# One load moved behind a group of DMA transposes: the sixth batch's v in a fused attention and mixer kernel

## The chip, the cores and the metric

The kernel runs on one core of a Trainium2 chip. The metric is device time in microseconds (us) of one execution; lower is better. Batches are numbered from 0 below, as in the code: the fifth batch is batch 4, the sixth is batch 5.

## The reference

For each of 8 batches and 8 heads (576 rows, head size 64) a linear attention with position weights is computed, then a mixer with two pairs of weights over all heads:

```python
phi(x) = concat(relu(x) * cos_w, relu(x) * sin_w)       # per row
kv  = phi(k).T @ v ;  z = sum(phi(k))
x   = (phi(q) @ kv) / (phi(q) @ z + 1e-6)               # 576 x 512 per batch, heads side by side
h   = relu(x.T @ w_tok1) @ w_tok2 ;  u = x + h.T        # token mixing, 576 -> 256 -> 576
out = u + relu(u @ w_ch1) @ w_ch2                       # channel mixing, 512 -> 1536 -> 512
```

## The kernel before

The 576 rows of a batch lie on 128 partitions in five pieces (j = 0 to 4); four are full and the fifth fills half of the partitions, two batches sharing one tail tile. Batches 0 and 1 and the preparation for 2 and 3 follow a list written out by hand. From batch 2 on there is a regular loop, one period for each batch p: the channel mixing of batch p (`channel`, L576 to L611) is TensorE's main work, and other batches' steps are hung into it at numbered slots. There are 12 slots after the first products (L589, tile `c_ps`) and 8 after the half sums of the second ones (L606, tile `o_ps`). In period p, `hooks_for(n, m, nxt)` hangs in:

- for batch n = p + 1: the kv product (slot 0, L361), the five numerators and their division (`numf`, L390, tile `nf`, slots 2 to 6; the division on DVE, L409 to L413), the token mixing (slots 7 to 8, L433), and the making of u (slots 10 to 12: `um` L460 and the addition L465 on DVE, the cast `ubc` to `ub` on POOL, the DMA transpose `utx` of `ub` into `uT`, L472, on SP; at slot 12 the tail, whose transpose for odd batches is L503)
- for batch m = p + 2: the casts of v to bf16 (`cast`, L264, on POOL, slots 3 to 7), the features of q on ACT (slots 9 to 13) and of k on DVE (slots 13 to 17), L330 and L332, and the DMA transposes `turnx` of the q features into `qpT`, L354 on SP: pieces 0 and 1 at slot 12, 2 and 3 at slot 15, 4 at slot 16
- for batch nxt = p + 3: the loads of k and q (slot 0) and of v (slot 9), L143 on SP, two DMAs each (512 and 640 KB), one for the even and one for the odd partitions

The stores of the output (L621, SP) come inside the second half of the channel mixing, two DMAs after j = 1 (between slots 14 and 15) and two after j = 3.

The order of calls is the order on each engine and queue: the schedule is manual, only the waits are put in by the framework. So SP issues its DMAs strictly in this order and each waits for its own data or buffer. Raw k and q have two buffers each, raw v one (L135 and below: `raw[t, 0 if t == "v" else b % 2]`), so a v load waits until the casts of the batch before it have read the buffer. `uT` and `qpT` have two buffers each.

Of the kernel before, what the change touches and what calls it, by code (L numbers as in the profile page):

```python
# [58 lines left out]
def kernel(  # L59
# [580 lines left out]
    def hooks_for(n, m, nxt):  # L640

        h = {}

        def at(slot, f, *a):
            h.setdefault(slot, []).append(lambda: f(*a))
        if nxt is not None:
            at(0, load, nxt, "k")
            at(0, load, nxt, "q")
            at(9, load, nxt, "v")
        if n is not None:  # L650
            at(0, n.kv_all)
            for j in range(JA):
                at(2 + j, n.num_all, j)
            for j in range(JA):
                at(7 + j // 3, n.mix, j, 2)
            at(8, n.mix_out)
            for g in range(3):
                at(10 + g, n.u_all, g)
        if m is not None:
            for j in range(JA):  # L660
                at(3 + j, m.cast, j, 1, 2, "P")
                at(9 + j, m.q_feature, j)
                at(13 + j, m.k_feature, j)
            at(12, m.turnx, 0, 2)
            at(15, m.turnx, 2, 2)
            at(16, m.turnx, 4, 1)
        return h

    evac = ["A"] * 7 + ["D", "A", "D", "D", "D"]
    for p in range(2, B):  # L670
        s = bt[p]
        n = bt[p + 1] if p + 1 < B else None
        m = bt[p + 2] if p + 2 < B else None
        nxt = p + 3 if p + 3 < B else None
        channel(s.uT, s.u, store_batch(p), evac if n else ["A", "D"] * 6, hooks_for(n, m, nxt))
# [33 lines left out]
```

## Time and profile before

| what | value |
|---|---|
| five runs | 274.94, 274.39, 274.09, 276.79, 274.52 us |
| median | 274.52 us |
| profiled execution | 274.94 us, of which the span of instructions is 273.2 us |
| busy in the span | PE 262.7, DVE 173.7, ACT 111.0, POOL 47.8 us |
| granted TensorE clock | 1.00 |
| DMA | 53.37 MB, mean 195 GB/s; 66.2% of 16 engines' span on SP's queue |

The periods of p = 2, 3, 4 and 5 start at 88.65, 116.24, 144.91 and 172.50 us of the span. All times inside the kernel below are counted from the start of the span. PE is TensorE's matmul, PEld its weight load, DVE VectorE, ACT ScalarE, POOL GpSimd; SPq is the queue of SyncE, whose times are those of issuing a DMA and not of its transfer. A DMA's landing is given as the time from issue to landing. Matmuls are pipelined, so the profile's durations of neighbours overlap a little.

### The profile page before, as it was taken

How to read it: one execution, taken by the hardware profiler on the slowest of the kernel's cores; microseconds unless marked ns; L12 is line 12 of the kernel's file. 1: busy time of each engine (PE TensorE's matmuls, PEld its weight loads, DVE VectorE, ACT ScalarE, POOL GpSimd, SP SyncE). 2: the span in 40 equal slices, each digit the busy share in tenths (PEclk: the TensorE clock that was granted, in tenths of full speed). 3: DMA queues.
4: the chain of work that ended last, by engine and by line, in shares of the span. 5: the costliest groups of instructions: out<-in, count | busy, mean ns of one | idle time of the engine just before them, and what ended most of it. 6: DMA issues, size and time to landing. Idle time of an engine off the chain costs nothing.

```text
span 273.2 us, 4855 instructions
## 1 busy us (share of the span) xinstructions
PE 262.7 (96%) x1923; PEld 137.9 (50%) x1941; DVE 173.7 (64%) x346; ACT 111.0 (41%) x176; POOL 47.8 (17%) x67
## 2 busy tenths in 40 slices
PE   6988999999999999999999999999999999999994
PEld 2775556455444644454445544554455444444443
DVE  6389788899982658945794669476837643424422
ACT  2786372565490548052903390339133201301300
POOL 2173060040060043500350026002000210000000
PEclk9999999999999999999999999999999999999999
DMA  6999999999999999999999958900980062012012
GB/s 205 358 233 174 288 229 254 356 175 248 382 220 220 317 382 359 195 218 302 334 179 241 352 164 179 230 30 3 219 204 2 0 155 97 0 46 107 2 66 89
DMA packets 79079, 53.37 MB, mean 195 GB/s; under 512 B 47824, under 2 KB 76496, under 8 KB 79056
## 3 DMA queue, kind: packets, MB, share of 16 engines
q1 hardware_dynamic: 74512, 48.77, 66.2%
q0 software_dynamic: 4144, 3.77, 9.1%
q10 hardware_dynamic: 400, 0.52, 0.5%
q8 instruction: 15, 0.25, 0.4%
q14 instruction: 8, 0.07, 0.1%
HBM read 35.85 MB, written 9.44 MB: 166 GB/s over the span
## 4 chain that ended last, share of the span: by engine, by line
PE 89%; DMA 5%; DVE 4%; issue 1%; DVEq 0%
PE o_ps L606 25%; PE c_ps L589 25%; PE c L512 8%; PE o L524 7%; PE b L433 6%; PE u L460 5%; PE kv L361 3%; DMA kt<-in_k_dram 3%; PE nf L390 3%; DMA qpT<-qp 2%; PE ut L488 1%; PE tr L345 1%; DVE kp L332 1%; PE o_ps L598 1%; PE nm L390 1%
## 5 line engine op out<-in xcount | busy, mean ns | idle before, releaser
L268 ACT ACTIVATE h<-c_ps 128x512 bf16<-128x512 f32 x52 | 31.0, 597 | 108.9 <-PE c_ps L589 65.3
L606 PE MATMUL o_ps<-wc,h 128*128 128x512 bf16 x317 | 71.5, 379 | 0.4
L589 PE MATMUL c_ps<-uT,wc 128*128 128x512 bf16 x288 | 70.4, 379 | 0.0
L606 PEld LDWEIGHTS <-h 128*128 128x128 bf16 x324 | 31.7, 98 | 38.2
L589 PEld LDWEIGHTS <-wc 128*128 128x128 bf16 x336 | 30.8, 98 | 32.6
L270 DVE TENSOR_SCALAR h<-c_ps 128x512 bf16<-128x512 f32 x32 | 22.0, 688 | 28.4 <-PE c_ps L589 28.4
L264 POOL CAST ub<-u 128x1024 bf16<-128x1024 f32 x14 | 14.9, 1067 | 108.6 <-issue 64.2
L330 ACT ACTIVATE qp<-qt,cos_t 128x512 bf16<-128x512 f32 x33 | 23.1, 713 | 11.8 <-DMA qt<-in_q_dram 11.5
L264 POOL CAST vbf<-vt 128x512 bf16<-128x512 f32 (+3 forms) x28 | 19.5, 731 | 48.0 <-DMA vt<-in_v_dram 46.7
L609 DVE TENSOR_TENSOR u<-o_ps,u 128x512 f32<-128x512 f32 x24 | 16.5, 688 | 17.5 <-PE o_ps L606 17.4
L512 PE MATMUL c<-uT,wc 128*128 128x512 bf16 x96 | 22.7, 379 | 0.1
L524 PE MATMUL o<-wc,h 128*128 128x512 bf16 x92 | 21.6, 379 | 0.2
L413 DVE TENSOR_TENSOR x<-nf,den 128x512 bf16<-128x512 f32 x30 | 20.7, 691 | 1.0
L332 DVE TENSOR_SCALAR kp<-kt,cos_t 128x512 bf16<-128x512 f32 x30 | 17.9, 599 | 5.5 <-DMA kt<-in_k_dram 5.5
L330 ACT ACTIVATE qp<-qt,sin_t 128x512 bf16<-128x512 f32 x30 | 21.1, 711 | 0.0
L465 DVE TENSOR_TENSOR u<-u,x 128x1024 f32<-128x1024 f32 x16 | 19.3, 1220 | 2.2 <-PE u L460 2.2
L390 PEld LDWEIGHTS <-qpT 128*128 128x128 bf16 x320 | 15.2, 98 | 10.7 <-DVE x L413 1.5
L433 PE MATMUL b<-x,w 128*128 128x512 bf16 (+1 forms) x84 | 19.8, 353 | 0.3
L332 DVE TENSOR_SCALAR kp<-kt,sin_t 128x512 bf16<-128x512 f32 x31 | 17.9, 583 | 0.0
L460 PE MATMUL u<-B,w 128*128 128x512 bf16 x64 | 16.1, 379 | 0.0
L409 DVE TENSOR_SCALAR den<-nf 128x8 f32<-128x8 f32 x30 | 5.0, 167 | 17.4 <-PE nf L390 17.3
L524 PEld LDWEIGHTS <-h 128*128 128x128 bf16 x96 | 9.1, 98 | 10.2
(92 smaller groups left out, 251.7 us busy)
## 6 DMA issues: line engine op xcount, KB each, us to landing
out_dram<-u SPq DMA_DIRECT2D x32, 256.0 KB, 2.7
qt<-in_q_dram SPq DMA_DIRECT2D x8, 640.0 KB, 7.1
kt<-in_k_dram SPq DMA_DIRECT2D x8, 640.0 KB, 8.0
qt<-in_q_dram SPq DMA_DIRECT2D x8, 512.0 KB, 6.0
kt<-in_k_dram SPq DMA_DIRECT2D x8, 512.0 KB, 6.9
vt<-in_v_dram SPq DMA_DIRECT2D x6, 640.0 KB, 9.7
vt<-in_v_dram SPq DMA_DIRECT2D x6, 512.0 KB, 8.7
wc<-in_moe_w_ch_dram POOLq DMA_DIRECT2D x4, 384.0 KB, 8.8
```

What stands on the lines that cost most here:

```text
L264: (nc.scalar.copy if eng == "A" else ENG[eng].tensor_copy)(dst, src)
L268: nc.scalar.activation(dst, src, AF.Relu)
L270: nc.vector.tensor_relu(dst, src)
L330: nc.scalar.activation(dst, src, AF.Relu, scale=tab)
L332: ENG[eng].tensor_scalar(dst, src, scalar1=tab, scalar2=0.0, op0=ALU.mult, op1=ALU.max)
L390: nc.tensor.matmul(nm[:, hh * (D + 1):(hh + 1) * (D + 1)], self.qpT[:, j * H + h, :], self.kv[:, h, :D + 1], start=(not eps or hh == 0), s ...
L433: nc.tensor.matmul(b1[:, mi], w1[:, col(self.c, j), mi * P:(mi + 1) * P], self.x[:, j, cs], start=(j == 0 and (g == 2 or mi == 0)), stop=( ...
L460: nc.tensor.matmul(ps[:, jj], w2[:, ki, 1 + 2 * g + jj, :], self.B1[:, ki, :], start=(ki == 0), stop=(ki == NT - 1))
L512: nc.tensor.matmul(ps, wc1[:, ki, mi * P:(mi + 1) * P], self.uT[:, :, ki, :], start=(ki == 0), stop=(ki == NCC - 1))
L524: nc.tensor.matmul(self.ps["o", j], self.h1[:, ki, j * P:(j + 1) * P], wc2[:, ki, :], start=(ki == 0), stop=(ki == NCH - 1))
L589: nc.tensor.matmul(c_ps, wc1[:, ki, mi * P:(mi + 1) * P], uT[:, :, ki, :], start=(ki == 0), stop=(ki == NCC - 1))
L606: nc.tensor.matmul(o_ps, h1[:, ki, j * P:(j + 1) * P], wc2[:, ki, :], start=(ki == 0), stop=(ki == NCH - 1))
```

## The change

In period p = 2 (nxt = 5, the sixth batch) the v load is no longer hung at slot 9 but at slot 16, after that slot's `turnx`. In periods 3 and 4 (nxt = 6 and 7) it stays at slot 9.

```diff
         if nxt is not None:
             at(0, load, nxt, "k")
             at(0, load, nxt, "q")
-            at(9, load, nxt, "v")
+            if nxt > 5:
+                at(9, load, nxt, "v")
         if n is not None:
             at(0, n.kv_all)
...
             at(12, m.turnx, 0, 2)
             at(15, m.turnx, 2, 2)
             at(16, m.turnx, 4, 1)
+        if nxt == 5:
+            at(16, load, nxt, "v")
         return h
```

On SP's queue the two DMAs of this load pass, in this order, the two `utx` of batch 3 (slots 10 and 11), its tail's transpose (slot 12), `turnx` of pieces 0 and 1 of batch 4's q, two stores of batch 2's output, and `turnx` of pieces 2 and 3 and of piece 4.

## The prediction

> **What bounds the kernel now.** I first read the page's busy shares: PE 262.7 of 273.2 us at a granted clock of 1.00, so time can be won only where PE pauses. The second view, busy time by stage, has one window for each period of the written-out loop (p = 2, 3, 4, 5); its columns are the stage, its length, the busy time of PE, PEld, DVE, ACT and POOL, the clock, the DMA share and GB/s.
>
> ```profile
> 88.65:116.24 27.59, 27.48 (x196) 13.87 (x196) 21.04 (x40) 12.51 (x20) 8.95 (x13) 1.00 1.08 313
> 116.24:144.91 28.67, 27.66 (x196) 13.79 (x196) 18.86 (x36) 12.51 (x20) 5.69 (x7) 1.00 1.02 258
> 144.91:172.50 27.59, 27.48 (x195) 13.91 (x196) 19.44 (x37) 12.51 (x20) 6.32 (x8) 1.00 0.86 236
> 172.50:200.08 27.58, 27.48 (x195) 13.90 (x196) 17.61 (x36) 12.51 (x20) 2.08 (x2) 1.00 0.57 116
> ```
>
> Three periods take 27.58 or 27.59 us and are full of PE work. Period 3 alone is 28.67, so 28.67 - 27.59 = 1.08 us can be won there. The chain of waits over 116 to 126 us says what ended last:
>
> ```profile
> 117.11 0.27 PE kv L361 x9
> 117.37 5.83 DMA qpT<-qp
> 123.20 0.05 issue
> 123.25 0.43 PE nf L390 x8
> ```
>
> The piece of 5.83 us is not a stall of 5.83 us: PE works beside it on other matmuls. The PE timeline shows the pause itself, in brackets:
>
> ```profile
> 121.31 1.02 PE L589 MATMUL c_ps<-uT,wc 128*128 128x512 bf16 x4
> 123.25 0.43 PE L390 MATMUL nf<-kv,qpT 128*128 128x65 bf16 x8 [0.91 <-DMA qpT<-qp]
> ```
>
> The first two numerators of period 3 (119.94 and 121.06) run in time; the third, due 123.25 - 1.08 = 122.17, needs row j = 2 of batch 4's transposed q, issued at 117.37 by turnx(2,2). Why so late? The timeline of SP's queue (start, us taken to issue):
>
> ```profile
> 97.04 2.96 SPq L143 DMA_DIRECT2D qt<-in_q_dram  x2
> 100.12 4.35 SPq L143 DMA_DIRECT2D vt<-in_v_dram  x2
> 106.17 6.01 SPq L472 DMA_TRANSPOSE uT<-ub  x2
> 112.28 1.23 SPq L503 DMA_TRANSPOSE uT_tail<-utb  x1
> 113.60 1.71 SPq L354 DMA_TRANSPOSE qpT<-qp  x1
> 115.40 1.88 SPq L621 DMA_DIRECT2D out_dram<-u  x2
> 117.37 5.13 SPq L354 DMA_TRANSPOSE qpT<-qp  x2
> 122.59 1.18 SPq L621 DMA_DIRECT2D out_dram<-u  x2
> ```
>
> The v load of batch 5 (the sixth) is issued at 100.12 into an already backed-up queue. By the DMA view of narrow windows its halves land 10.6 and 9.8 us after issue, at 110.7 and 112.4, and q's second half, issued at 99.40, lands 9.8 later, at 109.2. SP then needs 6.01 us to issue two u transposes, which elsewhere (162.43, period 4) take 2.90. Everything behind them slips.
>
> **The change, part by part.** Only two DMAs move (512 and 640 KB); nothing is added or removed. On SP they pass eight issues: two u transposes, the tail's, turnx(0,2), the store of j = 0 and 1, turnx(2,2), turnx(4,1). No instruction of POOL, PE, ACT or DVE moves.
>
> *The transposes come earlier.* Without v, the backlog ahead of the u transposes ends at 109.2 instead of 112.4, 3.1 us less. SP issues the first at 106.17 as before (its cast on POOL ends at 106.15), the second when its cast ends (107.82) and SP is free, the tail's after its cast (109.36). Then turnx(0,2) starts between 110.6 (an unhindered issue of 1.23 later) and 112.3, against 113.60; the store waits for DVE's u (111.10 + 0.69 = 111.79) and takes 1.58 to 1.88; so turnx(2,2) starts between 113.6 and 115.4, 2.0 to 3.8 us earlier than 117.37. With the 5.83 us that it took to land, row 2 is there at 119.4 to 121.2. Period 4, which has the same order and no backlog at its u transposes, agrees: turnx(2,2) starts at 170.62 and lands 5.9 later, 31.6 us after its period's start, which laid onto period 2 is 120.3. Due is 122.17, so 1.0 to 2.8 us are left over. turnx(4,1) landed at 124.4, its numerator then would be due at 124.42, and it too comes some 2 us earlier. What the stall yields is the smaller of 1.08 and the advance: 1.08 us, bounds 0 (nothing comes earlier) and 1.08 (PE has no other pause here).
>
> *The v load itself comes later.* turnx(4,1) ends between 116 and 119, so v starts at about 117.5. It queues behind the transposes and needs some 3.1 us of transfer, so it lands at about 124.5 (earliest 117.5 + the shortest v landing of the trace, 4.1; latest 119 + the longest, 10.6, = 129.6), instead of 112.36. Its reader:
>
> ```profile
> 112.47 3.42 POOL L264 CAST vbf<-vt 128x512 bf16<-128x512 f32 x5 [3.10 <-DMA vt<-in_v_dram]
> 133.77 1.04 POOL L264 CAST ub<-u 128x1024 bf16<-128x1024 f32 x1 [17.89 <-issue]
> ```
>
> POOL then idles 17.89 us until the u cast at 133.77 (132.69 after the gain), so casts that end at 124.5 + 3.42 = 127.9 stay inside this hole; latest 133.0, 0.3 us over. The kv matmuls that need them start at 145.6. Cost nothing; if the cover were gone, the u cast would come later by the excess. The casts lie now beside DVE's 1/den steps instead of the k features (0.87 us each beside them, 0.48 without). In period 2, batch 4's casts at 95.69 lie beside the same steps, whose products keep 0.69 us: nothing either.
>
> *Queued behind v on SP:* the store of j = 2 and 3, then k, q and v of batch 6 (123.82, 125.26, 126.68). They lose v's issue time (1.94 at most here) and gain the 2 to 3.8 us of the transposes. Batch 6's v writes the single raw v buffer, so SP waits for batch 5's casts: 127.9 instead of 126.68. Taken at its slowest, its second half issued at about 128.6 with the 10.3 us that it took before, it lands at 138.9 instead of 137.7, 1.2 later; k and q ahead of it are gone earlier, so I take 0. The u transposes of period 3 follow it on SP (134.84 and 136.73, landing 3.8 and 3.4 later, the last at 140.1) and are needed by the first matmul of period 4 at 144.74, 143.66 after the gain: 3.5 us of cover, from which the 1.2 would come.
>
> Two rules of the Trainium skill speak against this. "DMA: Bandwidth & Descriptors", section "Rules for kernel authors", says to issue a DMA early and wait for it late; by it alone the move gives up cover and the sum would stay at 274.94 or worse. The same page, "Queues, rings and completion order", says that completion is not first in, first out per issuing engine; by it the transposes might already overtake v, and the gain would be anything from 0 to 1.08. The rows speak otherwise: v's reader has a hole of 17.89 us, and the landings from 85 to 138 us came in the order of issue.
>
> Sum: the profiled execution took 274.94 us (273.2 span + 1.7 around it); 274.94 - 1.08 = 273.86. It lies 0.42 above the median of the five runs, 274.52; for a median the forecast is 273.44, rounded 273.4, or -0.39%.
>
> **The rivals.**
> 1. *The stall stays.* If SP's 6.01 us belong to the transposes and not to the backlog, turnx(2,2) starts at 117.4 again: 274.5. For: turnx(2,2) itself took 3.8 of the 5.13 us with no load just ahead. Against: 2.90 us for the same two issues in period 4.
> 2. *Slower: the late v holds up the next period's u.* The chain is v 5 -> casts on POOL -> buffer free -> SP waits with v 6 -> u transposes of batch 4 behind it -> first matmul of period 4. It decides where v 6 lands over 144.74 - 140.1 = 4.6 us later than before: issue after 131.3, casts begun after 127.9, that is v 5 landed 15.5 us later than at 112.4. I expect 12. If v keeps its 10.6 us from an issue at 122.5, it lands at 133.1, the casts end at 136.5, v 6 lands 10.3 later at 146.8, the u transposes at about 149.2: a stall of 149.2 - 144.7 = 4.5, so 279.0; halfway, about 277. Against: at 117 us only transposes and stores are ahead of it, at 100 the loads of k and q had not landed.
> 3. *Faster by more.* No row shows a second pause in period 3; only the scatter of the runs can carry -1.08 past -0.5%.
>
> **How the numbers follow.** 0.5%, or 1.37 us, is about what a measurement of this kernel can tell from no change; four of the five runs lie within 0.85 us. Chances: forecast 0.74, rival 1 0.13, rival 2 0.10, rival 3 0.03. The forecast lies 0.29 us short of the bound, so scatter takes a third of it (0.25) past: faster 0.25 + 0.03 = 0.28; same 0.49 + 0.13 + 0.01 of rival 2 = 0.63; slower 0.09. Range: below, 273.4 less the scatter, 272.7; above, rival 1 with its scatter, 274.9. Left out are most of rival 2 and a little of either end.
>
> **What would show it.** Right: period 3 at 27.6 us, no bracket before its third numerator; turnx(2,2) started by 115.4; the two u transposes issued in about 3 us instead of 6.01; POOL's casts of batch 5 at 122 to 130; batch 6's v issued at about 128. Wrong: 28.67 again (rival 1), or a PE pause near 144 for uT with POOL's casts begun after 127.9 (rival 2). A pause in period 3 before another numerator would mean that turnx(4,1) is late next.

## The result, and the profile after

The changed kernel takes 273.75 us in the median (31 runs) against 274.9 us for the kernel before (52 runs). The ratio is 0.9959 with a 95% interval of 0.9947 to 0.9971: about 1.1 us less, as forecast (1.08 us, or a ratio of 0.9961). The forecast median was 273.4, since it took the 1.08 us off a median of five runs, 274.52; over 52 runs the kernel before is 0.4 us longer than that. The profiled execution of the changed kernel took 274.43 us with a span of 272.7. That is only 0.5 us below the profiled execution of before, because its preparation, which the change does not touch, happened to run 0.59 us longer: period 2 starts at 89.24 us instead of 88.65. Times of the two profiles are therefore compared from the start of period 2, that is with 0.59 taken off those of after; for each of the runs below the first kv product of period 2 gives the shift.

Busy time by stage, one window for each of the periods 2 to 5 (columns as in the prediction: length, then PE, PEld, DVE, ACT, POOL, clock, DMA share, GB/s):

```profile
89.24:116.83 27.59, 27.48 (x195) 13.90 (x196) 19.72 (x40) 12.51 (x20) 5.54 (x8) 1.00 1.08 313
116.83:144.41 27.58, 27.48 (x195) 13.90 (x196) 18.68 (x36) 12.51 (x20) 8.53 (x12) 1.00 1.10 275
144.41:171.99 27.58, 27.48 (x195) 13.90 (x196) 19.44 (x37) 12.51 (x20) 6.32 (x8) 1.00 0.90 243
171.99:199.58 27.59, 27.48 (x196) 13.86 (x196) 17.61 (x36) 12.51 (x20) 2.08 (x2) 1.00 0.58 116
```

Period 3 is now as short as its neighbours. The five casts of v for batch 5 have moved from period 2 to period 3: POOL is busy for 5.54 instead of 8.95 us in the one and for 8.53 instead of 5.69 in the other, and no period is longer for it. The PE timeline around the third numerator has no bracket any more:

```profile
121.90 1.02 PE L589 MATMUL c_ps<-uT,wc 128*128 128x512 bf16 x4
122.76 0.42 PE L390 MATMUL nf<-kv,qpT 128*128 128x65 bf16 x8
```

SP's queue shows why:

```profile
98.35 2.96 SPq L143 DMA_DIRECT2D qt<-in_q_dram  x2
106.76 3.47 SPq L472 DMA_TRANSPOSE uT<-ub  x2
110.32 1.22 SPq L503 DMA_TRANSPOSE uT_tail<-utb  x1
111.63 1.78 SPq L354 DMA_TRANSPOSE qpT<-qp  x1
113.50 1.74 SPq L621 DMA_DIRECT2D out_dram<-u  x2
115.33 4.28 SPq L354 DMA_TRANSPOSE qpT<-qp  x2
119.67 2.14 SPq L143 DMA_DIRECT2D vt<-in_v_dram  x2
```

The two u transposes are issued in 3.47 instead of 6.01 us and turnx(2,2) starts at 115.33, which is 114.74 on the scale of before, 2.6 us earlier. Narrow windows of the DMA view give 6.5 us to its landing, at 121.8, where the numerator reads at 122.76: 0.97 us to spare.

### The profile page after: what moved, and what is told of

Read it like the earlier page. It is cut to its first block, busy times and chain, and to the rows that moved or that the text cites. A ratio compares the mean times of both kernels' runs of the same rounds, so it can differ in the third digit from the quotient of the medians.

```text
span 272.7 us, 4850 instructions
## 1 busy us (share of the span) xinstructions
PE 262.9 (96%) x1923; PEld 138.0 (51%) x1941; DVE 171.6 (63%) x346; ACT 110.9 (41%) x176; POOL 47.1 (17%) x67
## 4 chain that ended last, share of the span: by engine, by line
PE 84%; DMA 9%; DVE 3%; SPq 1%; issue 1%; POOL 1%; ACT 0%; DVEq 0%
PE c_ps L589 27%; PE o_ps L606 26%; PE o L524 7%; PE b L433 5%; PE c L512 5%; PE u L460 4%; DMA qt<-in_q_dram 4%; PE kv L361 3%; DMA wc<-in_moe_w_ch_dram 3%; PE nf L390 3%; DMA kt<-in_k_dram 2%; PE ut L488 1%; SPq L143 1%; PE o_ps L598 1%; DVE kp L332 1%
## 5 line engine op out<-in xcount | busy, mean ns | idle before, releaser
L606 PEld LDWEIGHTS <-h 128*128 128x128 bf16 x324 | 31.7, 98 | 38.2
L589 PEld LDWEIGHTS <-wc 128*128 128x128 bf16 x336 | 30.8, 97 | 32.6
L332 DVE TENSOR_SCALAR kp<-kt,cos_t 128x512 bf16<-128x512 f32 x30 | 17.2, 576 | 4.7 <-DMA kt<-in_k_dram 4.7
L512 PEld LDWEIGHTS <-wc 128*128 128x128 bf16 x96 | 8.9, 98 | 10.4 <-issue 1.2
```

What stands on the lines that cost most here:

```text
L332: ENG[eng].tensor_scalar(dst, src, scalar1=tab, scalar2=0.0, op0=ALU.mult, op1=ALU.max)
L512: nc.tensor.matmul(ps, wc1[:, ki, mi * P:(mi + 1) * P], self.uT[:, :, ki, :], start=(ki == 0), stop=(ki == NCC - 1))
L589: nc.tensor.matmul(c_ps, wc1[:, ki, mi * P:(mi + 1) * P], uT[:, :, ki, :], start=(ki == 0), stop=(ki == NCC - 1))
L606: nc.tensor.matmul(o_ps, h1[:, ki, j * P:(j + 1) * P], wc2[:, ki, :], start=(ki == 0), stop=(ki == NCH - 1))
```

## The experiments

Eleven runs were made: nine edited kernels, one of them twice, and the changed kernel again. The edits are shown against the kernel before except where stated. Each run is compared with runs of the kernel before on the same chip. "Pause" is PE's idle time in brackets before the third numerator of period 3, and period 3 is the time from the first kv matmul of period 3 to that of period 4.

| kernel | v of batch 5 is issued | pause, us | period 3, us | ratio (95% interval) |
|---|---|---|---|---|
| before | slot 9 | 0.91 | 28.67 | 1 |
| changed | slot 16 | none | 27.58 | 0.9959 (0.9947 to 0.9971) |
| x1_no_v5 | not at all | none | 27.58 | 0.9956 (0.9939 to 0.9973) |
| x2_half | 512 KB slot 9, 640 KB slot 16 | none | 27.58 | 0.9968 (0.9953 to 0.9983) |
| x3_pool_queue | slot 9, POOL's queue | 1.19 | 28.95 | 1.0001 (0.9973 to 1.0029) |
| x7_after_u | slot 11 | 0.68 | 28.44 | 0.9990 (0.9971 to 1.0009) |
| x11_half_before_turnx2 | 512 KB slot 14, 640 KB slot 16 | 0.23 | 27.98 | 0.9980 (0.9964 to 0.9997) |
| x5_before_turnx2 | slot 14 | 2.48 | 31.88 | 1.0079 (1.0050 to 1.0108) |

### Without the load, and half of it

```diff
 # x1_no_v5
-            at(9, load, nxt, "v")
+            if nxt > 5:
+                at(9, load, nxt, "v")
```

> Leaves out the v load of batch 5, so batch 5 is computed with batch 4's v; all else as before the change. My theory (the stall of period 3 comes from the v load standing ahead of the transposes, and its new place costs nothing): period 3 at 27.59 us, ratio to before 0.996, the same as the changed kernel's 0.9959 within 0.0015. Rival (the late v has a hidden price, so the changed kernel gives back a part of the gain): this one is clearly faster than the changed kernel, below 0.994. Rival 1 of the prediction (the transposes are slow by themselves): ratio 1.000, period 3 still 28.7 us. turnx(2,2) starts at 113.5 to 115.4 us after a period-2 start of 88.65.

The pause is gone and the ratio is that of the changed kernel. So the load ahead of the transposes is what held period 3 up, and in its new place it costs nothing that a comparison with its absence can find (0.9959 against 0.9956, whose interval is 0.0017, or 0.5 us, to either side). That the transposes were slow by themselves, rival 1 of the prediction, is refuted: without the load SP issues the two u transposes in 3.13 us instead of 6.01.

```profile
106.16 3.13 SPq L472 DMA_TRANSPOSE uT<-ub  x2
114.53 4.18 SPq L354 DMA_TRANSPOSE qpT<-qp  x2
```

```diff
 # x2_half: `load` is given a slice of its two DMAs
-            at(9, load, nxt, "v")
+            if nxt > 5:
+                at(9, load, nxt, "v")
+            else:
+                at(9, load, nxt, "v", slice(0, H), nc.sync, slice(0, 1))
...
             at(16, m.turnx, 4, 1)
+        if nxt == 5:
+            at(16, load, nxt, "v", slice(0, H), nc.sync, slice(1, 2))
```

> Only the second half of batch 5's v load (640 KB) moves to slot 16; the first half (512 KB) stays at slot 9. If the transposes advance in proportion to the bytes taken from ahead of them, the u transposes find a queue that is clear 0.55 x 3.1 = 1.7 us earlier, turnx(2,2) starts 1.1 to 2.1 us earlier than 117.37, and since the stall needs 1.08 us, it goes wholly or nearly: pause 0 to 0.3 us, ratio 0.996 to 0.997. If what counts is that no load at all is ahead (a threshold), the pause stays near 0.9 us and the ratio near 1.000.

Half of the load out of the way is enough: no pause. turnx(2,2) starts at 115.12 (115.4 on the scale of before, 2.0 us earlier, against 2.6 for the whole load), lands at 121.65, and its numerator at 121.91 does not wait, with 0.26 us to spare. Only the first 1.08 us of the advance can be used.

### SP's order or the bytes

```diff
 # x3_pool_queue
-            at(9, load, nxt, "v")
+            at(9, load, nxt, "v", slice(0, H), nc.gpsimd if nxt == 5 else nc.sync)
```

> Batch 5's v load keeps slot 9 but is issued from POOL's queue and not from SP's. The bytes come as early as before; only the place in SP's queue changes. If SP's own queue order is what delays the transposes: the two u transposes are issued in about 3.5 us instead of 6.01 and the pause of period 3 goes, ratio 0.996. If the bytes on the shared DMA engines are what delays them: the transposes still land late, pause 0.5 to 1.0 us, ratio 0.998 to 1.000. POOL's own work (u casts at 105 us) may be put back by the time it takes to issue, 1 to 2 us; that would show as a later start of the u transposes.

The load is out of SP's queue, and nothing is won. Timeline of SP, then of PE:

```profile
97.02 2.96 SPq L143 DMA_DIRECT2D qt<-in_q_dram  x2
105.92 6.35 SPq L472 DMA_TRANSPOSE uT<-ub  x2
...
117.41 5.23 SPq L354 DMA_TRANSPOSE qpT<-qp  x2
```

```profile
123.33 0.43 PE L390 MATMUL nf<-kv,qpT 128*128 128x65 bf16 x8 [1.19 <-DMA qpT<-qp]
```

On POOL's queue v lands at 106.4 and 108.7, but the second half of q, ahead on SP, now lands at 112.4 instead of 109.2. The same bytes occupy the same DMA engines, and SP again needs 6.35 us to issue the u transposes. So it is the bytes in front of the transposes that count, not whose queue they stand in. POOL's u casts were not put back (104.85 and 106.58), against my concern. The Trainium skill says as much in "DMA: Bandwidth & Descriptors", section "Issuing engines are not separate DMA queues": issuing on several engines saves only the time of the issue. This run agrees with it, with a pause of 1.19 us against 0.91, a little above the 0.5 to 1.0 that I had expected. Its twelve runs scatter from 273.29 to 276.81 us, and the shortest three, up to 273.59, are as short as runs of the changed kernel; whether the pause comes in every execution one trace cannot say.

### Other places ahead of turnx(2,2)

```diff
 # x7_after_u
-            at(9, load, nxt, "v")
+            if nxt > 5:
+                at(9, load, nxt, "v")
...
                 at(10 + g, n.u_all, g)
+            if nxt == 5:
+                at(11, load, nxt, "v")
```

> Batch 5's v load moves only behind the two u transposes (slot 11), ahead of the tail's transpose and of all three turnx. If what counts is how many bytes stand ahead of turnx(2,2) and when they start: v now starts at about 110.3, when the DMA engines run dry (they moved 10 to 70 GB/s at 115 us before the change), so most of its 3 us of transfer falls into that hole; turnx(2,2) starts at 116 to 117.5 and lands at 122 to 124 against 122.8 due, a pause of 0 to 1.1 us, ratio 0.996 to 1.000. If any place ahead of turnx is as bad as slot 9: pause 1.1 us or more, ratio 1.000 or above.

```diff
 # x5_before_turnx2
-            at(9, load, nxt, "v")
+            at(14 if nxt == 5 else 9, load, nxt, "v")
```

> Batch 5's v load moves only from slot 9 to slot 14: behind the u transposes and turnx(0,2), but still ahead of turnx(2,2) on SP. If being ahead of turnx(2,2) is what costs (its issue and its 3 us of transfer): turnx(2,2) starts about 2 us later than in the changed kernel (at 117.2 instead of 115.3) and lands at 124 to 126 where 122.8 is due, a pause of 1 to 3 us in period 3, ratio 1.000 to 1.008. If only the jam at the u transposes costs (SP's 6.01 us): no pause, ratio 0.996.

```diff
 # x11_half_before_turnx2: as x2_half, but its first half at slot 14
-                at(9, load, nxt, "v", slice(0, H), nc.sync, slice(0, 1))
+                at(14, load, nxt, "v", slice(0, H), nc.sync, slice(0, 1))
```

> The first half of batch 5's v load (512 KB) stands at slot 14, ahead of turnx(2,2), the second half at slot 16. With both halves at slot 14 the pause was 2.48 us, after it TensorE's granted clock was 0.50 for 3.4 us, and period 3 was 4.3 us long over 27.59. If the pause goes by the bytes ahead of turnx(2,2): about 1.1 us here (the changed kernel's margin of 1.0 us less 0.45 of the 3.5 us that the whole load put turnx(2,2) back), pause 0.3 to 1.3 us. If the clock drops only behind a long pause: it stays at 1.00, period 3 is over by no more than the pause, ratio 0.998 to 1.001. If any pause drops it: period 3 is over by the pause plus 1.7 us, ratio above 1.004.

In all three the jam at the u transposes is gone (x5_before_turnx2 and x7_after_u issue both in 2.90 us), and still there is a pause. SP's queue in x5_before_turnx2:

```profile
105.79 2.90 SPq L472 DMA_TRANSPOSE uT<-ub  x2
...
112.13 1.84 SPq L143 DMA_DIRECT2D vt<-in_v_dram  x2
114.07 1.23 SPq L621 DMA_DIRECT2D out_dram<-u  x2
115.39 7.26 SPq L354 DMA_TRANSPOSE qpT<-qp  x2
```

The chain of waits gives the landing of turnx(2,2), and the PE timeline the pause behind it:

```profile
115.39 9.00 DMA qpT<-qp
```

```profile
124.44 0.43 PE L390 MATMUL nf<-kv,qpT 128*128 128x65 bf16 x8 [2.48 <-DMA qpT<-qp]
```

On the scale of before, turnx(2,2) starts at 115.8, 1.0 us later than in the changed kernel, and lands at 124.7, 3.5 us later. So the time at which SP starts the issue accounts for 1.0 of the 3.5 us. The other 2.5 are a longer landing, 9.0 us instead of 6.5, with the v load ahead of it and only two stores, which the changed kernel has too, in between. In x7_after_u it is the other way round: turnx(2,2) starts 2.4 us later than in the changed kernel (117.2) and lands in 5.8 us, which leaves a pause of 0.68. That a part of v's transfer there fills time in which the engines would be idle (in the changed kernel they move 50 to 93 GB/s from 112 to 113 us) is argued and not shown. Half the load at slot 14 gives a landing of 7.4 us and a pause of 0.23, just under the expected 0.3 to 1.3; the whole load there gives 2.48. No place ahead of turnx(2,2) that was tried for the whole load is free of a pause. With the pause of 0.23 us the clock stayed at 1.00.

The 2.48 us had a second price. Period 3 is 31.88 - 27.58 = 4.3 us too long, 1.7 to 1.8 more than the pause. Busy time by stage during the pause and behind it (the third number from the end of each line is the clock):

```profile
122.00:124.40 2.40, 0.00 (x0) 0.00 (x0) 0.26 (x1) 0.59 (x1) 0.25 (x1) 1.00 1.19 226
124.40:126.40 2.00, 1.96 (x17) 1.06 (x18) 1.06 (x3) 0.04 (x1) 0.00 (x0) 0.65 0.99 315
126.40:128.40 2.00, 2.00 (x14) 0.90 (x12) 1.06 (x3) 0.55 (x1) 0.00 (x0) 0.50 0.97 300
128.40:130.40 2.00, 1.95 (x17) 1.05 (x17) 1.54 (x4) 0.60 (x1) 0.00 (x0) 0.99 1.05 371
```

The clock is at half speed for (0.35 x 2 + 0.50 x 2 + 0.01 x 2) / 0.5 = 3.4 us, which loses 1.7 us of PE work. Of the six runs of this kernel four have a mean clock of 0.991 or 0.992 and take 277.74 to 278.62 us, the traced one among them; two have 0.997, as runs of the kernel before also have, and take 276.18 and 276.76. So the drop seems not to come in every execution, and the ratio of 1.0079 is a mixture; the two have no trace that could show their pause.

### Still later: the slower rival

```diff
 # x4_after_kq
             at(0, load, nxt, "q")
-            at(9, load, nxt, "v")
+            if nxt == 6:
+                at(0, load, 5, "v")
+            if nxt > 5:
+                at(9, load, nxt, "v")
```

> Batch 5's v load is issued still later, in period 3 behind the k and q loads of batch 6 and just ahead of v of batch 6. This goes past the point from which rival 2 of the prediction decides. Rival 2's chain: v 5 lands about 8 us later than in the changed kernel (135.7 instead of 127.9), its casts end at 138.6, the u casts on POOL and v 6 on SP come behind them (u casts at 138.6 instead of 133.3, v 6 issued at 138.6 instead of 130.9), the u transposes land at 145.5 to 147 instead of 141.35, and TensorE pauses some 2 to 3 us at the first matmul of period 4 (144.2): ratio 1.002 to 1.009, that is slower than the changed kernel by 2 to 3 us. If the lateness of v were harmless, ratio 0.996 as in the changed kernel.

```diff
 # x8_v6_late_too: as x4_after_kq, and batch 6's v behind turnx of period 3
-            if nxt > 5:
+            if nxt > 6:
                 at(9, load, nxt, "v")
...
             at(16, m.turnx, 4, 1)
+        if nxt == 6:
+            at(16, load, nxt, "v")
```

> As in x4_after_kq, batch 5's v comes in period 3 behind k and q of batch 6, but batch 6's v load goes to slot 16 of that period, behind the transposes. This cuts the SP link of rival 2's chain (SP waiting with v 6 ahead of the u transposes) and leaves the POOL link (u casts behind the casts of v). If the SP link carried the cost: u casts still at about 136.3, but the u transposes are issued at 137.4 and 138.5 and land by 142.5, before the 143.4 at which x4_after_kq's first matmul of period 4 was due; no pause, ratio 0.996. If the POOL link carried it: the pause of about 1.1 us at uT stays, ratio 1.000 or above.

The late v does what rival 2 said, and makes the kernel slower. In x4_after_kq POOL's casts end at 136.3 and hold up the u casts; on SP v of batch 6 waits for them (its two DMAs are issued at 136.3 and 137.0) with the u transposes behind it; and period 4 begins with a pause:

```profile
133.44 2.85 POOL L264 CAST vbf<-vt 128x512 bf16<-128x512 f32 x5 [24.48 <-DMA vt<-in_v_dram]
136.24 2.22 POOL L264 CAST ub<-u 128x1024 bf16<-128x1024 f32 x2
```

```profile
144.52 1.02 PE L589 MATMUL c_ps<-uT,wc 128*128 128x512 bf16 x4 [1.10 <-DMA uT<-ub]
```

A second pause of 0.36 us follows at a numerator of period 4, since turnx is late as well. By the first kv products period 3 is 1.26 us and period 4 0.55 us over 27.58, together 1.8. The ratio is 1.0038 (1.0016 to 1.0060), that is 0.0079 x 274.7 = 2.2 us slower than the changed kernel, inside the expected 2 to 3. The pause itself, 1.1 us, is shorter than the 2 to 3 that I had expected: v landed at 133.3, which is 134.2 on the scale of the changed kernel, and not at 135.7.

In x8_v6_late_too the u casts are as late (136.78) but the u transposes have nothing ahead of them; they land by 142.9 and period 3 is 27.58 us with no pause. Timeline of SP, x4_after_kq first:

```profile
137.73 4.66 SPq L472 DMA_TRANSPOSE uT<-ub  x2
```

```profile
138.09 2.63 SPq L472 DMA_TRANSPOSE uT<-ub  x2
```

On the scale of before both start at 138.1 to 138.2; but the two land 5.6 and 5.3 us after their issue in x4_after_kq and 3.3 and 3.4 in x8_v6_late_too. So it was v of batch 6 ahead of the u transposes that turned the lateness into a pause, and by the transfer in front of them, not by a later start on SP; POOL's late casts alone cost nothing. The expectation of no pause at all was a miss: in its place v of batch 7 comes late, since it waits for batch 6's casts. It is issued at 159.55, just ahead of the next u transposes, and the picture of period 2 of the kernel before is there again two periods on.

```profile
159.55 1.28 SPq L143 DMA_DIRECT2D vt<-in_v_dram  x2
161.27 6.14 SPq L472 DMA_TRANSPOSE uT<-ub  x2
```

```profile
178.21 0.43 PE L390 MATMUL nf<-kv,qpT 128*128 128x65 bf16 x8 [0.78 <-DMA qpT<-qp]
```

Its ratio, 0.9925 (0.9898 to 0.9952, six runs), is nevertheless as low as those without any pause. The profiled execution, 274.29 us, is the second longest of the six (272.67 to 274.40), so this pause may come in some executions only; that was not settled.

### The same move for all three batches, and the changed kernel again

```diff
 # x6_all_late and x10_all_late_again
-            at(9, load, nxt, "v")
...
             at(16, m.turnx, 4, 1)
+        if nxt is not None:
+            at(16, load, nxt, "v")
```

> All three v loads of the loop (batches 5, 6 and 7) are issued at slot 16 of their periods, behind turnx. If the move pays only where TensorE pauses: periods 3 and 4 had no pause, so nothing more is won, ratio 0.996 (within 0.0015 of the changed kernel), periods of 27.58 throughout. If the late loads hold something up in periods 4 and 5 (casts on POOL ahead of the u casts), a pause there and a ratio above 0.998.

> The kernel with all three v loads late once more, since its ratio (0.9931) came out lower than the changed kernel's (0.9959) with intervals that overlap, while its profile has the same periods of 27.58 us. If there is nothing more to win than the pause: the same ratio as the changed kernel of this call, within 0.0015. If the later loads win something that the profile does not show: lower by 0.002 or more again.

> The changed kernel once more, beside the all-late one on the same chip. If the gain is the 1.08 us pause and nothing else: ratio 0.996 (0.9945 to 0.9975), no pause behind 85 us. It also shows by a second profile how far turnx(2,2) lands ahead of its reader (1.0 us in the first).

With all three late there is no pause and the periods stay at 27.57 to 27.59 us. The first ratio, 0.9931 (0.9908 to 0.9954), looked lower than that of the changed kernel, by more than the expected 0.0015; on one chip the two came to 0.9934 (0.9912 to 0.9956) and 0.9946 (0.9926 to 0.9965), which differ by 0.0012 and cannot be told apart. The preparation alone moves the start of period 2 by up to 1.05 us between the profiles (its first kv product at 88.89 to 89.94), so ratios of a few runs are less sharp here than the lengths of the periods. So no version was found that is shown to beat the changed kernel; behind period 2 there is no pause left in it to win. In its second profile turnx(2,2) lands at 121.4, 0.9 us ahead of its reader at 122.26, and v of batch 5 at 126.0, which is 1.4 us earlier than in the first when both are counted from the start of period 2.

## Why the prediction was right

**The stall (1.08 us).** Right in size and cause. The bound was read from one period against its neighbours, not from the 5.83 us of the chain's piece, and period 3 went from 28.67 to 27.58. x1_no_v5 shows that the load's old place cost no more than this.

**The advance.** Right, at its late end. The u transposes were said to take about 3 us to issue and took 3.47; turnx(2,2) was to start between 113.6 and 115.4 and started at 114.74; it was to land between 119.4 and 121.2 and landed at 121.2, since it needed 6.5 us and not the 5.83 of before. Of the 1.0 to 2.8 us that should be left over, 0.97 were.

**The reason for the advance.** The prediction spoke of SP's queue and of the backlog as of one thing. x3_pool_queue, x5_before_turnx2 and x7_after_u part them: the bytes in front of the transposes are the cause. SP's long issues come with them (6.35 us with v on POOL's queue, 2.90 with v behind the u transposes), and a later start on SP is a part of the delay, 1.0 of 3.5 us in x5_before_turnx2.

**The late v.** Costless as said, but the margins were mis-sized. It was to be issued at about 117.5 and to land at 124.5; on the scale of before it was issued at 119.1 and landed at 127.3, because turnx(2,2) and turnx(4,1) took 4.28 us to issue and the load then 5.8 and 6.8 us to land. The casts began at 127.5 and v of batch 6 was issued at 130.3 instead of 127.9, 1.0 us short of the point that I had worked out for rival 2 (131.3). That point was worked out with the first matmul of period 4 at 144.74; with 143.66, where the gain puts it and which the prediction used for the cover, it would have been 130.2, and so by its own sum the changed kernel stood at the edge of rival 2. It did not come to that because v of batch 6 landed faster than the sum had it. Its second half was issued 2.3 us later than forecast and landed 7.9 us after its issue instead of 10.3; that it landed at 138.9, exactly the "slowest" of the prediction, is two errors that cancel, and luck. The last u transpose landed at 140.8, 2.9 us ahead of the first matmul of period 4, so 0.7 us of cover were used where I took 0. The casts do not lie beside the division on DVE as forecast: its last product ends at 126.6 and they begin at 128.0 (both in the changed kernel's profile), so what they would do to it was not tested. They took 2.84 us there instead of 3.42; the k features that they left behind all take 0.48 us now.

**Rival 2.** The mechanism is real (x4_after_kq), though its link on SP worked by the transfer of v of batch 6 and not by SP's wait; the weak term was its price. It assumed that v of batch 6 takes 10.3 us to land, as it did in a full queue; issued so late, it found the queue empty and landed 4.4 and 5.5 us after its issue. For a v landed at 133.3 the cost was a pause of 1.1 us and a second one of 0.36, and not 4.5. What the prediction left out in the other direction is the clock: the one pause of 2.48 us cost 1.7 us more than itself.

**The two rules of the skill** that spoke against the change did not decide. The early issue was not needed here: POOL, which reads v, had 17.89 us of idle time, of which 2.40 are left before its next u cast. And a completion out of order, by which the transposes might have overtaken v in the kernel before, was not seen on SP's queue in any of these profiles around the change. Between two queues it was: in x3_pool_queue the second half of v, issued on POOL's at 99.5, landed at 108.7, ahead of the second half of q, issued on SP's at 99.3 and landed at 112.4.

## What to carry to other kernels

When a DMA with a near deadline (here a transpose that feeds the next products) shares the engines with a load that nobody needs for a whole period, count the bytes that stand ahead of it, also on another queue; move the load behind the urgent one and check that its reader, and the next load into the same buffer, still have cover. The worth of such a move is the pause of the bounding engine, here a period against its neighbours, and the rest of the advance is only margin: half the move removed the same pause. Check the chain through a single buffer as well: a load that waits for its buffer can put its bytes just ahead of the next urgent transfer, as v of batch 6 did in x4_after_kq and v of batch 7 in x8_v6_late_too.

## What the runs showed of the hardware that was not expected

A pause of TensorE of 2.48 us in otherwise dense work was followed by 3.4 us at a granted clock of 0.50 (x5_before_turnx2, one trace; the mean over that profile is 0.992, and four of its six runs have such a mean), and pauses of 0.23, 0.36, 0.68, 0.78, 0.91, 1.10 and 1.19 us, one trace each, were not; there the clock stayed at 1.00 in the windows behind them. The Trainium skill, "TensorE: Matmul & The Clock Gate", Part 1, gives an idle window of about 3.4 us as what brings the half clock back; here a shorter pause was enough, and the measurement decides. Where between 1.19 and 2.48 us it turns, and whether that depends on more than the length of the pause, is open.
